# Causal attention and expert layer on one core: part of the diagonal mask as constant rows of the score product, and one f16 piece of the row maxima

## The chip, the cores and the metric

One Trainium2 chip, one core of it. The metric is the device time of one launch in microseconds (us). Each kernel is one program with one launch; 775.1 us is the median of three runs of the kernel before (772.79 to 777.4).

## What is computed

Eight batches of eight heads, 576 positions, head size 64, in f32; then a layer of eight experts with a capacity of 576 tokens each, routed by the largest remaining logit.

```python
scores = scale * np.matmul(q, k.transpose(0, 1, 3, 2))
causal = np.triu(np.ones((S, S), dtype=bool), k=1)
cum = np.cumsum(np.maximum(s, 0.0), axis=-1)
bias = -(cum[:, :, :, None] - cum[:, :, None, :])
scores = np.where(causal, -1000000000.0, scores + np.minimum(bias, 0.0))
scores = scores - np.max(scores, axis=-1, keepdims=True)
attn = np.exp(scores)
attn = attn / (np.sum(attn, axis=-1, keepdims=True) + 1e-09)
return np.matmul(attn, v).astype(np.float32)
...
logits = x @ w_gate          # x: the attention output, 4608 tokens of 512
h = np.maximum(x[mask] @ w1[e], 0.0)
out[mask] = h @ w2[e]        # for each expert e and the tokens given to it
```

## The kernel before

**Order of the work.** Every instruction is a task of a planner (class Plan, L90 on): it has an engine (t = TensorE, a = ScalarE, v = VectorE, p = GpSimd, s = the SyncE queue of transfers), a guessed duration, tasks that must come first, buffers from rings, and a priority (smaller goes first). The planner plays the engines through and gives out the instructions in the order in which they start in that play; each engine then runs its own list strictly in that order, waiting on semaphores. A change of one duration or one task so changes the order of the whole attention phase. Tasks marked `lock` are played so that one on VectorE and one on GpSimd don't overlap. A transfer marked `bulk` starts only when the backlog of transfers in the play (270 KB per us) has come down to 0.8 us. The expert phase has a plan of its own that the diff doesn't touch.

**Attention.** The 64 heads go in 16 groups g of four heads, each group in two pairs pr of two heads ("par" 0 and 1), so 32 pairs, numbered n0 = 2g + pr. For each group `load` (L363) brings q and k, scales them and splits them into a high and a low f16 part. They lie in one of four ring slots of the tile QK, `[128, 2, 2, 2, HB]` in f16 (partitions, plane, q or k, pair, 1280 columns). Partitions 0 to 63 of plane 0 hold the high parts; partitions 64 to 69 of plane 0 hold six more rows that enter the same product: three pieces of the running sums (the bias), two pieces of the row maximum and one constant. Plane 1 holds the cross products of high and low parts on all 128 partitions. Partitions 70 to 127 of plane 0 are not used.

**First pass** (`spass`, L459): scores from 67 rows of plane 0 alone, whose row maxima VectorE takes in ten steps (L471) into mr. The ten maxima of a row go through ScalarE as f16 into mp (L518) and as f32 into ms (L520); GpSimd takes the difference as the second f16 piece (L522); TensorE turns mp over (L524), ScalarE copies it out as mt of 20 rows (L526), and a transfer (L529) lays it into rows 67 and 68 of plane 0.

**Second pass** (`sts`, L533): the transposed scores, keys in the partitions and queries in the columns, 512 columns at a time (`unit`). Each piece of columns is one product over 70 rows of plane 0 (L544) plus one over 128 rows of plane 1 (L545), summed in PSUM; a block on the diagonal gets a third one, 128 columns of the identity times the mask mT (L547), which adds -1e9 where the key is later than the query:

```python
def mm(ps, c0, n, ks, q, diag=False):
    nc.tensor.matmul(ps[:, c0:c0 + n], F()[:, ks:ks + 128], F()[:, q:q + n], start=True, stop=False)
    nc.tensor.matmul(ps[:, c0:c0 + n], G()[:, ks:ks + 128], G()[:, q:q + n], start=False, stop=not diag)
    if diag:
        nc.tensor.matmul(ps[:, c0:c0 + 128], self.identb, self.mT, start=False, stop=True)
```

There are four diagonal blocks for each head: as the first 128 of 512, of 384 and of 256 columns, and one of 128 alone. ScalarE takes the exponential into P (L555), GpSimd writes what bf16 leaves of it into R (L557). `pv` (L592) multiplies with V in three products for each block (L618 to L620), `norm` (L631) divides (VectorE L644, L645, L649), `turn` (L662) transposes the result (L681) and adds it to the router logits (L692, L693). L411 and L444 are VectorE's low parts of q, k and v. At the start 70 products of zeros (L735) run on TensorE, and `consts` (L248) makes the constants, most of them on GpSimd.

**Experts.** After the last pair the router finishes, and eight experts run one after the other (lines from L840 on).

Of the kernel before, what the change touches and what calls it, by code (L numbers as in the profile page):

```python
# [42 lines left out]
OH = 704  # L43
# [173 lines left out]
class Attention:  # L217
# [30 lines left out]
    def consts(self):  # L248
# [17 lines left out]
        self.wgf = T([128, 4, E], F32, "wgf")  # L266
        self.vec = T([128, 2], F32, "vec")
# [10 lines left out]
        zrow = self.mZ.bitcast(F16)[64:70, None, 0:HB // 2].to_broadcast([6, 4, HB // 2])  # L278
        for i in range(4):
            t = self.r["QK"].slots[i][0]  # L280
            p0 = -97 if i == 0 else 2 * i - 5.6
            rows, made = t[64:70, 0], []
            if i < 2:
                for c in (1, 0):
                    made.append(pl.add("v", 0.85, lambda rows=rows, c=c: nc.vector.tensor_scalar(
                        rows[:, c].rearrange("p r (h c) -> p (r h) c", h=2), zrow, self.vec[64:70, c:c + 1], None,
                        op0=OP.add), [k["vec", 0, 4], k["vec", 1, 1], k["mZ"]], prio=p0 if c or i else -94, lock=True))
            else:

                made.append(pl.add("p", 0.9, lambda rows=rows: nc.gpsimd.dma_start(rows, self.r["QK"].slots[1][0][64:70, 0]),  # L290
                                   self.rows1 + [k["QK", 1]], prio=-20, kb=62))
# [167 lines left out]
    def spass(self, g, pr):  # L459
# [69 lines left out]
        st["max", pr] = pl.add("s", 0.67, lambda: nc.sync.dma_start(to.t[67:69, 0, 0, pr], mt.t), [x], prio=n0 - 2.9,  # L529
                               uses=[mt, QK], kb=5, alt=("a", 0.62, lambda: nc.scalar.dma_start(  # L530
                                   to.t[67:69, 0, 0, pr], mt.t)) if n0 < 4 else None)

    def sts(self, g, pr):  # L533
# [7 lines left out]
        ready = [k["ib"], k["mT1"], k["mU1", 0], k["mU1", 64], st["max", pr]] + st["pass"][pr][0] + st["pass"][pr][1] + st["st"][pr]  # L541
# [20 lines left out]
        for m, (par, j) in enumerate(((0, 0), (0, 1), (0, 2), (1, 0), (1, 1), (1, 2))):  # L562
            o, t = self.q0(par, pr, 0), self.q0(par, pr, 4) + 64 * par
            kk = lambda ki, par=par: self.k0(par, pr) + 128 * ki
            if j == 0:
                go = lambda ps, o=o, kk=kk: mm(ps, 0, 512, kk(0), o, True)
                dur = 2 * T_(512) + T_(128)
            elif j == 1:
# [4 lines left out]
                dur = 4 * T_(64) + 2 * T_(384) + T_(128)  # L573
            else:
# [5 lines left out]
                dur = 4 * T_(64) + 2 * T_(256) + 4 * T_(128)  # L580
# [136 lines left out]
    def build(self):  # L717
# [5 lines left out]
        self.sums()  # L723
        self.gate()
# [747 lines left out]
```

## Time and profile before

| what | value |
|---|---|
| three runs, median (lowest to highest) | 775.1 us (772.79 to 777.4) |
| the profiled execution's own time | 777.66 us |
| its span, first to last instruction | 775.6 us |
| TensorE (PE) busy | 722.0 us, 93% |
| VectorE (DVE) busy | 598.2 us, 77% |
| ScalarE (ACT) busy | 391.7 us, 50% |
| GpSimd (POOL) busy | 335.3 us, 43% |
| transfers | 118.72 MB, mean 153 GB/s |
| mean granted TensorE clock | 0.964 of 2.4 GHz |

A busy matmul in the profile includes the modelled time until its result has drained, so that successive matmuls overlap: their price is read from start to start. PEld is the loading of a matmul's weights, POOL is GpSimd, SPq the queue of the SyncE engine, from which most transfers are issued. Idle time in brackets is that of the engine just before the instruction, with what ended it.

### The profile page before, as it was taken

How to read it: one execution, taken by the hardware profiler on the slowest of the kernel's cores; microseconds unless marked ns; L12 is line 12 of the kernel's file. 1: busy time of each engine (PE TensorE's matmuls, PEld its weight loads, DVE VectorE, ACT ScalarE, POOL GpSimd, SP SyncE). 2: the span in 40 equal slices, each digit the busy share in tenths (PEclk: the TensorE clock that was granted, in tenths of full speed). 3: DMA queues.
4: the chain of work that ended last, by engine and by line, in shares of the span. 5: the costliest groups of instructions: out<-in, count | busy, mean ns of one | idle time of the engine just before them, and what ended most of it. 6: DMA issues, size and time to landing. Idle time of an engine off the chain costs nothing.

```text
span 775.6 us, 22590 instructions
## 1 busy us (share of the span) xinstructions
PE 722.0 (93%) x8726; PEld 454.9 (59%) x8726; DVE 598.2 (77%) x2014; ACT 391.7 (50%) x794; POOL 335.3 (43%) x428
## 2 busy tenths in 40 slices
PE   9789999999999999628998999999999999999995
PEld 3457788787888888416644544545445454454542
DVE  7889999999999996678895877969788795380110
ACT  3548888888888878405334323324244232461110
POOL 7648988788878988102032041140412224202011
PEclk9679999999999999858999999999999999999998
DMA  7897768686776511106157376394845639851000
GB/s 233 195 213 202 220 175 250 172 241 196 209 203 171 156 35 64 63 35 204 42 167 200 110 113 180 129 222 133 190 156 155 187 105 262 228 180 48 15 28 34
DMA packets 89733, 118.72 MB, mean 153 GB/s; under 512 B 39246, under 2 KB 55758, under 8 KB 89614
## 3 DMA queue, kind: packets, MB, share of 16 engines
q1 hardware_dynamic: 83116, 97.82, 46.1%
q0 software_dynamic: 5952, 19.00, 8.1%
q8 instruction: 68, 1.11, 0.6%
q10 hardware_dynamic: 558, 0.47, 0.2%
q14 instruction: 39, 0.32, 0.1%
HBM read 71.67 MB, written 19.10 MB: 117 GB/s over the span
## 4 chain that ended last, share of the span: by engine, by line
PE 54%; issue 19%; DVE 13%; DMA 5%; POOL 4%; ACT 2%; SPq 1%; POOLq 0%; ACTq 0%; DVEq 0%
PE psm L1293 13%; PE psm L1379 10%; DVE pss L471 5%; PE pst L545 4%; PE pst L544 4%; PE pss L502 3%; PE po L618 3%; PE po L620 2%; PE po L619 2%; POOL out_dram L1352 2%; POOL xg L1226 2%; PE psn L1297 2%; PE po L735 2%; PE pss L681 2%; DMA xg<-xs,ids 1%
## 5 line engine op out<-in xcount | busy, mean ns | idle before, releaser
L557 POOL TENSOR_TENSOR R<-P 128x512 f16<-128x512 f32 (+1 forms) x221 | 218.9, 1016 | 26.9 <-ACT P L555 25.2
L1293 PE MATMUL psm<-xT,w1p 128*128 128x512 f16 (+1 forms) x876 | 193.1, 353 | 1.3 <-DMA xT<-xg 0.8
L1379 PE MATMUL psm<-w2p,hT 128*128 128x512 f16 x768 | 174.4, 379 | 0.0
L555 ACT ACTIVATE P<-pst 128x512 f32<-128x512 f32 (+1 forms) x224 | 119.9, 555 | 25.0 <-PE pst L547 10.3
L1297 PE MATMUL psn<-xT,w1p 128*128 128x64 f16 x768 | 129.7, 193 | 0.0
L471 DVE CUSTOM_DVE_ANT_0 pss<-pss,mS 128x512 f32<-128x512 f32 (+3 forms) x256 | 122.7, 506 | 9.0 <-PE pss L502 8.0
L1293 PEld LDWEIGHTS <-w1p 128*128 128x128 f16 x876 | 79.2, 98 | 80.0 <-issue 1.9
L1352 POOL DMA_INDIRECT out_dram<-y,ids x40 | 39.8, 995 | 198.7 <-ACT y L1390 169.6
L1379 PEld LDWEIGHTS <-hT 128*128 128x128 f16 x768 | 69.0, 98 | 80.3 <-issue 4.4
L1226 POOL DMA_INDIRECT xg<-xs,ids x40 | 43.6, 1089 | 167.3 <-DVE ids L1184 67.3
L618 PE MATMUL po<-V,P 128*128 128x65 f16 x960 | 113.8, 196 | 1.4 <-DVE xp L649 1.0
L620 PE MATMUL po<-V,R 128*128 128x65 f16 x960 | 114.0, 194 | 0.4 <-POOL R L557 0.4
L619 PE MATMUL po<-Vl,P 128*128 128x64 f16 x960 | 113.6, 193 | 0.0
L544 PE MATMUL pst<-QK 70*128 70x64 f16 (+4 forms) x512 | 108.5, 252 | 1.2 <-ACT P L555 0.7
L545 PE MATMUL pst<-QK 128*128 128x64 f16 (+4 forms) x512 | 107.8, 251 | 0.0
L619 PEld LDWEIGHTS <-P 128*128 128x128 bf16 x960 | 90.0, 100 | 9.1 <-issue 2.8
L618 PEld LDWEIGHTS <-P 128*128 128x128 bf16 x960 | 90.4, 98 | 5.9 <-issue 1.8
L1313 ACT ACTIVATE hT<-psm 128x512 f16<-128x512 f32 x64 | 38.2, 597 | 108.1 <-PE psm L1293 88.3
L620 PEld LDWEIGHTS <-R 128*128 128x128 f16 x960 | 89.9, 97 | 0.6 <-POOL R L557 0.6
L1390 ACT ACTIVATE y<-psm 128x512 f32<-128x512 f32 x32 | 19.1, 597 | 122.0 <-PE psm L1379 108.1
L502 PE MATMUL pss<-QK 67*128 67x512 f16 (+3 forms) x256 | 72.6, 307 | 4.7 <-DVE mr L471 2.4
L1297 PEld LDWEIGHTS <-w1p 128*128 128x128 f16 x768 | 67.7, 98 | 1.3
(221 smaller groups left out, 1443.4 us busy)
## 6 DMA issues: line engine op xcount, KB each, us to landing
QK<-QK SPq DMA_DIRECT2D x120, 144.0 KB
wst<-in_w_dram SPq DMA_DIRECT2D x32, 512.0 KB
wst<-in_w_dram SPq DMA_DIRECT2D x64, 256.0 KB
raw<-in_q_dram SPq DMA_DIRECT2D x32, 288.0 KB
raw<-in_k_dram SPq DMA_DIRECT2D x32, 288.0 KB
rv<-in_v_dram SPq DMA_DIRECT2D x32, 288.0 KB
xs<-xp SPq DMA_DIRECT2D x32, 256.0 KB
xs<-xp SPq DMA_DIRECT2D x8, 128.0 KB
```

Of the source, the lines that this page charges most:

```text
L471: return pl.add("v", dur, lambda: nc.vector.tensor_tensor_reduce(ps(), ps(), mask, 1.0, init() if init else -3e38, OP.add, OP.max, mr.t[:, ...
L502: nc.tensor.matmul(ps.t[:, :n], F()[:, q0:q0 + 128], F()[:, k0:k0 + n], start=True, stop=True)
L544: nc.tensor.matmul(ps[:, c0:c0 + n], F()[:, ks:ks + 128], F()[:, q:q + n], start=True, stop=False)
L545: nc.tensor.matmul(ps[:, c0:c0 + n], G()[:, ks:ks + 128], G()[:, q:q + n], start=False, stop=not diag)
L555: e = pl.add("a", n / 1200 + 0.171, lambda: nc.scalar.activation(P.t[:, c0:c0 + n], ps.t[:, :n], AF.Exp, scale=1.0 / YS), [x] + fresh, pri ...
L557: sub = lambda eng: eng.tensor_tensor(R.t[:, c0:c0 + n], P.t[:, c0:c0 + n], strided_hi(P.t)[:, c0:c0 + n], op=OP.subtract)
L618: nc.tensor.matmul(o[:, i], H[:, c:c + 128], V.t[:, pr, sl], start=f, stop=False)
L619: nc.tensor.matmul(o[:, i, 0:64], H[:, c:c + 128], Vl.t[:, pr, sl], start=False, stop=False)
L620: nc.tensor.matmul(o[:, i], R.t[:, c:c + 128], V.t[:, pr, sl], start=False, stop=l)
L1293: nc.tensor.matmul(ps[:, tiles[0]:tiles[-1] + 1] if len(tiles) > 1 else ps[:, tiles[0]], lhs(f, c, a), xT.t[:, tiles[0]:tiles[-1] + 1, 4 * ...
L1297: nc.tensor.matmul(pt.t[:, 64 * f:64 * f + 64], lhs(f, c, a), xT.t[:, 4, 4 * b + c, 0:64], start=s, stop=e)
L1379: nc.tensor.matmul(py.t, hT.t[:, f, a, 128 * i:128 * i + 128], w2p.t[:, f, b], start=f == 0 and k == 0, stop=f == 7 and k == 2)
```

## The change

From the fifth group on (g >= 4, 24 of the 32 pairs), partitions 72 to 127 of plane 0 hold constants in all four slots: on the key side 65504 where the row's number is smaller than the key's (mA), on the query side -65504 where row and query have the same number (mB). Their product, summed over these 56 rows, is about -4.3e9 wherever the key is later than one of the first 56 queries of a block. The diagonal 128 columns are now a product of their own over all 128 partitions of plane 0, the columns after them a second one over 70, and the mask product is left with the last 72 of its 128 columns. The constants are made by four GpSimd instructions and brought into the slots by 16 transfers of 56 partitions by 2 KB. In all 32 pairs the row maximum goes as one f16 piece: the f32 copy, the difference and the second row are gone. Partitions 64 to 71 instead of 64 to 69 are filled at the start, with one more select for each of two columns of vec.

```diff
+HUGE, MR = 65504.0, 72
...
-            mr=R(w, [128, 10], F32, "mr", 3), ms=R(w, [128, 10], F32, "ms", 2), mp=R(w, [128, 128], F16, "mp", 2),
-            mt=R(w, [20, 128], F16, "mt", 2),
+            mr=R(w, [128, 10], F32, "mr", 3), mp=R(w, [128, 128], F16, "mp", 2), mt=R(w, [10, 128], F16, "mt", 2),
...
+            P(("vec", c), 0.2, lambda v=v: g.affine_select(
+                v, v, pattern=[[0, 1]], base=5, channel_multiplier=-1, compare_op=OP.is_ge, fill=0.0), -99, [("vec", c, len(rows))])
...
+    def rows(self):
+
+        nc, pl, k, g = self.nc, self.pl, self.k, self.nc.gpsimd
+        x = None
+        for t, v, op, base, fill in ((self.mA, HUGE, OP.is_ge, 63 + MR - 64, 0.0), (self.mB, 0.0, OP.not_equal, MR, -HUGE)):
+            x = pl.add("p", 0.5, lambda t=t, v=v: g.memset(t, v), [x], prio=1.5)
+            x = pl.add("p", 0.6, lambda t=t, op=op, base=base, fill=fill: g.affine_select(
+                t, t, pattern=[[0, 4], [1, 128]], base=base, channel_multiplier=-1, compare_op=op, fill=fill), [x], prio=1.5)
+        for i in range(4):
+            q = self.r["QK"].slots[i][0][MR:128, 0]
+            made = []
+            for t, (src, o1) in enumerate(((self.mB, OH + 64), (self.mA, OH))):
+                for o in (0, o1):
+                    made.append(pl.add("s", 0.6, lambda q=q, t=t, o=o, src=src: nc.sync.dma_start(
+                        q[:, t, :, o:o + 512], src[MR:128].rearrange("p i c -> p (i c)")[:, None].to_broadcast([128 - MR, 2, 512])),
+                        [x], prio=2.5 + i, kb=115, bulk=True))
+            k["rows", i] = made
...
-        a2 = pl.add("a", 0.21, lambda: nc.scalar.activation(ms.t.rearrange("p (a b) -> p a b", a=2), both(), AF.Copy, scale=1.0 / YS), done,
-                    prio=n0 - 2.9, uses=[mr, ms])
-        p1 = pl.add("p", 0.2, lambda: nc.gpsimd.tensor_sub(mp.t[:, 10:20], ms.t, mp.t[:, 0:10]), [a1, a2], prio=n0 - 2.9, lat=0.35,
-                    uses=[ms, mp])
...
-                   [p1, k["i16b"]], prio=n0 - 2.9, uses=[ps, mp])
-        x = pl.add("a", 0.25, lambda: nc.scalar.activation(mt.t, ps.t.bitcast(F16)[0:20, 0:128], AF.Copy), [x], prio=n0 - 2.9,
+                   [a1, k["i16b"]], prio=n0 - 2.9, uses=[ps, mp])
+        x = pl.add("a", 0.25, lambda: nc.scalar.activation(mt.t, ps.t.bitcast(F16)[0:10, 0:128], AF.Copy), [x], prio=n0 - 2.9,
...
+        new = g >= 4
+        F1 = lambda: self.flat(QK.t, slice(0, 128), 0)
...
         def mm(ps, c0, n, ks, q, diag=False):
-            nc.tensor.matmul(ps[:, c0:c0 + n], F()[:, ks:ks + 128], F()[:, q:q + n], start=True, stop=False)
+            m = 128 if diag and new else 0
+            if m:
+                nc.tensor.matmul(ps[:, c0:c0 + m], F1()[:, ks:ks + 128], F1()[:, q:q + m], start=True, stop=False)
+            if n > m:
+                nc.tensor.matmul(ps[:, c0 + m:c0 + n], F()[:, ks:ks + 128], F()[:, q + m:q + n], start=not m, stop=False)
             nc.tensor.matmul(ps[:, c0:c0 + n], G()[:, ks:ks + 128], G()[:, q:q + n], start=False, stop=not diag)
             if diag:
-                nc.tensor.matmul(ps[:, c0:c0 + 128], self.identb, self.mT, start=False, stop=True)
+                z = 128 - MR if new else 0
+                nc.tensor.matmul(ps[:, c0 + z:c0 + 128], self.identb, self.mT[:, z:], start=False, stop=True)
...
+        TM = T_(128) - (0.0233 if new else 0.0)
+        TB = TM + (0.003 if new else 0.0)
```

In `sts` the planner's durations of the units with a diagonal block use TB and TM instead of T_(128), and the tasks of a group from the fifth on also wait for the constants of their slot.

## Rows read from the trace of the kernel before

**Rows 1.** Busy time by stretch: length, PE, PEld, DVE, ACT, POOL (counts), clock, DMA share, GB/s.
```profile
20.00:60.00 40.00, 32.42 (x326) 21.25 (x324) 34.94 (x105) 21.57 (x44) 22.41 (x31) 0.74 0.89 205
60.00:100.00 40.00, 39.00 (x756) 31.89 (x754) 39.19 (x134) 34.43 (x83) 34.72 (x38) 1.00 0.76 212
100.00:240.00 140.00, 138.28 (x2683) 113.89 (x2682) 137.85 (x455) 120.93 (x277) 114.14 (x128) 1.00 0.72 205
240.00:300.00 60.00, 60.00 (x1198) 49.86 (x1196) 54.85 (x188) 48.79 (x120) 51.59 (x58) 1.00 0.37 109
```
**Rows 2.** Matmuls of L524, one for each pair, counted in two stretches.
```profile
100.00:240.00 140.00, 3.50 (x16) 1.56 (x16) 1.00 0.72 205
240.00:300.00 60.00, 1.54 (x7) 0.68 (x7) 1.00 0.37 109
```
**Rows 3.** The chain of waits within 100 to 240 us, shares by line.
```profile
by line: DVE pss L471 11.7%; PE pst L545 9.8%; PE pst L544 9.6%; PE pss L502 9.0%; PE po L618 7.0%; PE po L620 6.3%; PE po L619 6.2%; issue 4.7%; DVE Vl L444 4.6%; PE pss L681 4.0%; DVE po L645 3.5%; DVE QK L411 3.3%; PE pss L486 3.3%; PE p
```
**Rows 4.** The chain of waits within 240 to 300 us, shares by line.
```profile
by line: PE pst L545 15.9%; PE pst L544 15.7%; PE pss L502 12.1%; PE po L618 11.5%; PE po L620 10.7%; PE po L619 10.6%; PE pss L681 7.0%; PE pss L486 5.6%; PE pst L547 5.2%; PE po L692 1.6%; PE po L693 1.3%; PE pst L588 0.7%; PE pst L587 0.
```
**Rows 5.** TensorE's timeline, 165 to 168 us: start, duration, instruction.
```profile
165.56 0.38 PE L544 MATMUL pst<-QK 70*128 70x512 f16 x1
165.78 0.38 PE L545 MATMUL pst<-QK 128*128 128x512 f16 x1
166.00 0.22 PE L547 MATMUL pst<-mT,identb 128*128 128x128 bf16 x1
...
167.15 0.44 PE L681 MATMUL pss<-ident,xp 128*128 128x128 f16 x5
167.43 0.19 PE L618 MATMUL po<-V,P 128*128 128x65 f16 x1
```
**Rows 6.** Groups by form, 100 to 240 us: count, busy us, mean ns, idle before.
```profile
L557 POOL TENSOR_TENSOR R<-P 128x512 f16<-128x512 f32 x96 | 102.3, 1090 | 9.2 <-ACT P L555 8.9
...
L411 DVE SCALAR_TENSOR_TENSOR QK<-raw,QK 128x1152 f16<-128x1152 f32 x16 | 22.9, 1433 | 0.0
...
L547 PEld LDWEIGHTS <-identb 128*128 128x128 bf16 x128 | 12.5, 98 | 6.5
...
L522 POOL TENSOR_TENSOR mp<-ms,mp 128x10 f16<-128x10 f32 x16 | 7.4, 460 | 16.6 <-ACT ms L520 11.3 <-PE pss L486 4.3 <-PE pst L545 1.0
...
L520 ACT ACTIVATE ms<-mr 128x10 f32<-128x10 f32 x16 | 3.3, 205 | 0.0
```
**Rows 7.** VectorE's timeline, 134 to 138 and 160 to 170 us.
```profile
135.18 1.67 DVE L444 SCALAR_TENSOR_TENSOR Vl<-rv,V 128x1152 f16<-128x1152 f32 x1
136.78 0.48 DVE L649 TENSOR_TENSOR xp<-po,xp 128x320 f16<-128x320 f32 x1
...
163.09 1.31 DVE L411 SCALAR_TENSOR_TENSOR QK<-raw,QK 128x1152 f16<-128x1152 f32 x1
```
**Rows 8.** TensorE's timeline at 137 us; in brackets the idle time before.
```profile
137.31 0.19 PE L618 MATMUL po<-V,P 128*128 128x65 f16 x1 [0.61 <-DVE xp L649]
```
**Rows 9.** GpSimd's timeline, 0 to 60 us.
```profile
12.70 1.76 POOL L831 TENSOR_SCALAR_AFFINE_SELECT qb<-on 128x128 f16<-128x128 f16 x4
...
21.46 0.21 POOL L522 TENSOR_TENSOR mp<-ms,mp 128x10 f16<-128x10 f32 x1 [6.14 <-ACT ms L520]
```
**Rows 10.** The chain of waits within 14 to 60 us: start, length, what.
```profile
13.79 2.16 PE po L735 x10
...
26.72 6.87 DMA QK<-QK
...
49.28 5.94 DMA raw<-in_q_dram
...
56.37 0.25 ACT mt L526
```
**Rows 11.** The SyncE queue's timeline, 55 to 57 us.
```profile
55.23 0.36 SPq L382 DMA_DIRECT2D raw<-in_k_dram  x1
55.86 0.96 SPq L440 DMA_DIRECT2D rv<-in_v_dram  x2
```

More of the change, by code (lines that the diff above doesn't have):

```diff
@@ L266, in consts @@
         self.wgf = T([128, 4, E], F32, "wgf")
+        self.mA, self.mB = T([128, 4, 128], F16, "mA"), T([128, 4, 128], F16, "mB")
         self.vec = T([128, 2], F32, "vec")
@@ L281, in consts @@
             p0 = -97 if i == 0 else 2 * i - 5.6
-            rows, made = t[64:70, 0], []
+            rows, made = t[64:MR, 0], []
             if i < 2:
@@ L285, in consts @@
                     made.append(pl.add("v", 0.85, lambda rows=rows, c=c: nc.vector.tensor_scalar(
-                        rows[:, c].rearrange("p r (h c) -> p (r h) c", h=2), zrow, self.vec[64:70, c:c + 1], None,
-                        op0=OP.add), [k["vec", 0, 4], k["vec", 1, 1], k["mZ"]], prio=p0 if c or i else -94, lock=True))
+                        rows[:, c].rearrange("p r (h c) -> p (r h) c", h=2), zrow, self.vec[64:MR, c:c + 1], None,
+                        op0=OP.add), [k["vec", 0], k["vec", 1], k["mZ"]], prio=p0 if c or i else -94, lock=True))
             else:
-                made.append(pl.add("p", 0.9, lambda rows=rows: nc.gpsimd.dma_start(rows, self.r["QK"].slots[1][0][64:70, 0]),
+                made.append(pl.add("p", 0.9, lambda rows=rows: nc.gpsimd.dma_start(rows, self.r["QK"].slots[1][0][64:MR, 0]),
                                    self.rows1 + [k["QK", 1]], prio=-20, kb=62))
@@ L509, in spass @@
                 extra.append(tri(9, At(ps, 384, 448), self.mC, 64, x, prio, more=[k["mC1", 0], k["mC1", 64]]))
-        ms, mp, mt, ps = (self.buf(n) for n in ("ms", "mp", "mt", "pst" if n0 < 2 else "pss"))
+        mp, mt, ps = (self.buf(n) for n in ("mp", "mt", "pst" if n0 < 2 else "pss"))
         fresh = [k["mp", n0]] if n0 < 2 else []
@@ L519, in spass @@
                     prio=n0 - 2.9, uses=[mr, mp])
-        a2 = pl.add("a", 0.21, lambda: nc.scalar.activation(ms.t.rearrange("p (a b) -> p a b", a=2), both(), AF.Copy, scale=1.0 / YS), done,
-                    prio=n0 - 2.9, uses=[mr, ms])
-        p1 = pl.add("p", 0.2, lambda: nc.gpsimd.tensor_sub(mp.t[:, 10:20], ms.t, mp.t[:, 0:10]), [a1, a2], prio=n0 - 2.9, lat=0.35,
-                    uses=[ms, mp])
         x = pl.add("t", 0.06, lambda: nc.tensor.transpose(ps.t.bitcast(F16)[:, 0:128], mp.t, self.ident16),
-                   [p1, k["i16b"]], prio=n0 - 2.9, uses=[ps, mp])
-        x = pl.add("a", 0.25, lambda: nc.scalar.activation(mt.t, ps.t.bitcast(F16)[0:20, 0:128], AF.Copy), [x], prio=n0 - 2.9,
+                   [a1, k["i16b"]], prio=n0 - 2.9, uses=[ps, mp])
+        x = pl.add("a", 0.25, lambda: nc.scalar.activation(mt.t, ps.t.bitcast(F16)[0:10, 0:128], AF.Copy), [x], prio=n0 - 2.9,
                    uses=[ps, mt])
         to = QK
-        st["max", pr] = pl.add("s", 0.67, lambda: nc.sync.dma_start(to.t[67:69, 0, 0, pr], mt.t), [x], prio=n0 - 2.9,
+        st["max", pr] = pl.add("s", 0.67, lambda: nc.sync.dma_start(to.t[67:68, 0, 0, pr], mt.t), [x], prio=n0 - 2.9,
                                uses=[mt, QK], kb=5, alt=("a", 0.62, lambda: nc.scalar.dma_start(
-                                   to.t[67:69, 0, 0, pr], mt.t)) if n0 < 4 else None)
+                                   to.t[67:68, 0, 0, pr], mt.t)) if n0 < 4 else None)
     def sts(self, g, pr):
@@ L540, in sts @@
         fresh = [k["P", n0], k["R", n0]] if n0 < 2 else []
-        ready = [k["ib"], k["mT1"], k["mU1", 0], k["mU1", 64], st["max", pr]] + st["pass"][pr][0] + st["pass"][pr][1] + st["st"][pr]
+        new = g >= 4
+        F1 = lambda: self.flat(QK.t, slice(0, 128), 0)
+        ready = (k["rows", g % 4] if new else []) + [k["ib"], k["mT1"], k["mU1", 0], k["mU1", 64], st["max", pr]] + st["pass"][pr][0] + st["pass"][pr][1] + st["st"][pr]
         def mm(ps, c0, n, ks, q, diag=False):
-            nc.tensor.matmul(ps[:, c0:c0 + n], F()[:, ks:ks + 128], F()[:, q:q + n], start=True, stop=False)
+            m = 128 if diag and new else 0
[3 more added lines that the diff above has]
+                nc.tensor.matmul(ps[:, c0 + m:c0 + n], F()[:, ks:ks + 128], F()[:, q + m:q + n], start=not m, stop=False)
             nc.tensor.matmul(ps[:, c0:c0 + n], G()[:, ks:ks + 128], G()[:, q:q + n], start=False, stop=not diag)
             if diag:
-                nc.tensor.matmul(ps[:, c0:c0 + 128], self.identb, self.mT, start=False, stop=True)
+                z = 128 - MR if new else 0
+                nc.tensor.matmul(ps[:, c0 + z:c0 + 128], self.identb, self.mT[:, z:], start=False, stop=True)
         T_ = lambda n: n / 2400 + 0.003
+        TM = T_(128) - (0.0233 if new else 0.0)
+        TB = TM + (0.003 if new else 0.0)
         st["e", pr] = {}
@@ L566, in sts @@
                 go = lambda ps, o=o, kk=kk: mm(ps, 0, 512, kk(0), o, True)
-                dur = 2 * T_(512) + T_(128)
+                dur = 2 * T_(512) + TB
             elif j == 1:
@@ L572, in go @@
                     mm(ps, 448, 64, kk(1), t)
-                dur = 4 * T_(64) + 2 * T_(384) + T_(128)
+                dur = 4 * T_(64) + 2 * T_(384) + TB
             else:
@@ L579, in go @@
                     mm(ps, 448, 64, kk(3), t)
-                dur = 4 * T_(64) + 2 * T_(256) + 4 * T_(128)
+                dur = 4 * T_(64) + 2 * T_(256) + 2 * T_(128) + TB + TM
             unit((par, j), (par * PW + 512 * j, 512), dur, go, [], n0 + m / 7)
@@ L723, in build @@
         self.sums()
+        self.rows()
         self.gate()
```

2 lines of the change are left out of this document (1 added, 1 removed).

## Prediction

> **What bounds the kernel now.** I read the busy time by stretch first [rows 1]: between 60 and 300 us TensorE is at full clock and nearly always busy, VectorE too up to 240 us, GpSimd at 82 to 87%; the stretch up to 60 us has the transfers at 89% of their engines and a clock of 0.74. Busy shares don't tell which of two full engines decides, so next comes the pace. Each pair has one L524, 16 in 140 us and 7 in 60 us [rows 2]: 8.75 us a pair up to 240 us, 8.57 us after. The chain of waits says why: after 240 us it consists of TensorE alone [rows 4]; up to 240 us [rows 3], of the shares that are shown, the TensorE lines make 55.2% and VectorE's (L471, L444, L645, L411) 23.1%. So 8.57 us is what TensorE needs for a pair, and the 0.18 us above it is waiting for VectorE. One such wait: GpSimd and VectorE hold each other up, a two-input step of VectorE takes 1.31 us when free and 1.67 us here, so the L649 behind it is late [rows 7], and the L618 that needs the buffer finds TensorE idle for 0.61 us [rows 8]. Before 60 us the chain runs through transfers [rows 10]. The expert phase isn't touched and only moves.
>
> **Shorter masks.** 24 pairs times 8 diagonal blocks are 192 mask products. In a stream a matmul costs its columns at 2.4 GHz and a little more: 512 columns start 0.22 us apart (213.3 ns of columns), five of 128 take 0.28 us, 56 ns each (53.3 ns) [rows 5]. Going from 128 to 72 columns takes off 56 columns, 23.3 ns, in all 4.48 us of TensorE.
>
> **Split products.** Three of the four diagonal blocks of a head are cut off from a longer product, so 24 x 2 x 3 = 144 matmuls are new, with no new columns. Each costs the part above its columns, 2.7 ns by the 128-column row, 6.7 ns by the 512-column row [rows 5]; I take 5 ns, 0.72 us. Its weight load, 98 ns in its row [rows 6], must hide: the five transposes start 56 ns apart, each with weights of its own [rows 5], so loads overlap and I add nothing. 128 rows for 70 in the diagonal product: L544 over 70 rows and L545 over 128 rows both take 0.22 us from start to start [rows 5], so nothing. Net 3.76 us of TensorE (3.5 to 4.1), 0.157 us a pair.
>
> The row thus prices a 128-column matmul with its own weights at 56 ns. The Trainium skill (TensorE: Matmul & The Clock Gate, "Back-to-back issue gap") says that in a stream of weight loads and matmuls the spacing is set by both, about 81 ns at 128 columns and 131 ns at 512, which would make the splits dear; the trace disagrees at both ends, with 56 and 220 ns.
>
> **What of it reaches the end.** The eight pairs 24 to 31 run where the chain is TensorE alone: 8 x 0.157 = 1.25 us. Of the 16 changed pairs before them, which run in about the stretch of [rows 3] (2.51 us), I count two thirds, about TensorE's part of the chain (55.2 of 78.3) with something off for VectorE, which is then late sooner: 1.67 us. Together 2.9 us. The ends are 1.25 us (nothing where VectorE stands on the chain) and 3.76 us (all).
>
> **One piece of the maxima.** ScalarE loses L520, 0.205 us a pair [rows 6]; it is at 86% [rows 1] and on no chain that I show above, so nothing. GpSimd loses L522, 0.46 us a pair with its waits, and 1.04 us a pair of standing idle ahead of it while the R of L557, 1.09 us each, queue behind [rows 6]. No row shows TensorE waiting for an R, so directly nothing. Indirectly it moves when GpSimd and VectorE collide: L411 took 1.433 us on average against 1.31 us free [rows 6, 7], 16 x 0.123 = 2.0 us of blocking between 100 and 240 us; that can go or double, and nothing says which: 0, with 2.0 us either way in the range. The shorter way to the row of maxima could matter only before 60 us, where the chain is transfers [rows 10]: 0; at most the 0.205 + 0.46 us of the two steps for each of the first four pairs, 2.7 us.
>
> **Another order.** New durations and missing tasks shift every engine's list. The 16 x 0.18 = 2.9 us above TensorE's pace is what an order can give back or lose again: 0, with 2.9 us either way.
>
> **Constants.** Four GpSimd instructions: four selects of 128 columns take 1.76 us [rows 9], so a select of 512 about as much, and a fill no more: under 7.0 us, nearer 4. Their priority 1.5 puts them ahead of the router's constants (3), whose end is followed by 6.14 us of idle GpSimd [rows 9]: hidden; uncovered it would cost up to 0.9 us. The two selects for vec, at most 0.44 us each by the same row, stand ahead of the first loads' rows; the chain at 14 us is still in the zero products of L735 [rows 10], so hidden, 0 to 0.9 us.
>
> **Sixteen transfers.** 56 rows x 2 x 1 KB are 0.115 MB, in all 1.84 MB. From 60 to 100 us the transfers move 212 GB/s at a share of 0.76 [rows 1], so full engines would move 279 GB/s and need 6.6 us for them; the free 24% of those 40 us is 9.6 us. From 20 to 60 us, at 0.89, only 4.4 us are free, and at that stretch's 205 GB/s over 0.89 they need 8.0 us. Which stretch? The first slot's priority is 2.5; the q and k of the fifth group (1.0) and the v of the fourth (1.5) go first, and these were issued at 55.23 and 55.86 us [rows 11]; the other slots (3.5 and later) also stand behind the sixth group's q and k (3.0). So after 57 us, ahead of the first use, in the ninth pair: 0. The price if not is a rival below. On SP each issue is some 0.4 us and waits for constants long made.
>
> **Sum.** 777.66 - 2.9 = 774.8 us against the profiled execution's own time, which lies 2.56 us above the median of the runs; from the median, 772.2 us.
>
> **Rivals.**
> *VectorE paces.* It is busy 98% of 100 to 240 us [rows 1], and nothing is taken off it. Then only the last eight pairs gain: 775.1 - 1.25 = 773.9 us. Against: some of that busy time is blocking, and TensorE leads the chain.
> *The blocking goes too.* Without L522 GpSimd and VectorE collide less, and the first 16 pairs come down to TensorE's new pace: 16 x (0.18 + 0.157) + 1.25 = 6.6 us, 768.5 us. For: the 16.6 us of idle ahead of L522 [rows 6]. Against: L557 blocks as before.
> *Slower, by the transfers.* Place: 20 to 60 us. Constants are ready early, and where the planner's 270 KB per us empties a backlog that the chip still has, rows go out ahead of q, k and v. The chain there is a QK transfer of 6.87 us and a load of 5.94 us, behind which ScalarE's queue held L526 up to 56.37 us [rows 10]. Price: 8.0 - 4.4 = 3.6 us of transfers too many, up to all 8.0 us if they stand ahead of the load on the chain. It decides from 2.9 us on, what the masks give; at 6 us it is 775.1 + 3.1 = 778.2 us. A TensorE idle longer there also stays at the half clock longer.
> *Slower, by weight loads.* If the 98 ns of a load [rows 6] stood open for each of the 144 splits, 14.1 us would go against 4.48 us: 784.7 us. The 56 ns of [rows 5] speak against it. By the page named above the splits would also cost more than the masks give.
> *Not what it says.* 65504 squared over the scale of 8192 is an exponent near -520,000, so the mask holds and the time is as summed.
>
> **How the numbers follow.** Forecast 45% (its own range 770.3 to 774.5); VectorE paces 20%; blocking goes 17%; transfers 14%; weight loads 2%; 2% for an order that is worse by more. What a measurement of this kernel can tell from no change is about 0.5%, 3.9 us: under 771.2 or over 779.0 us. Under it lie a third of the forecast's spread by reordering (15%), nearly all of the case without blocking (16%) and a little of the rest (5%): 0.36. Over it lie over half of the transfers' case (8%) and the last two (4%): 0.12. The range takes in the gain without blocking and part of what early transfers cost: 767.5 to 778.0 us.
>
> **What would show it.** After 240 us the pace falls from 8.57 to 8.41 us a pair and the mask products are 33 ns apart (72 columns and 3 ns); in 100 to 240 us it falls to about 8.65 us, with VectorE still on the chain. The sixteen transfers are issued after 57 us and the chain before 60 us is as it was. It is wrong if the pace after 240 us stays, if diagonal products of 128 columns start much over 58 ns apart, if the first 60 us grow by microseconds, or if the pace before 240 us falls by more than TensorE's 0.157 us.

## Result and profile after

| | kernel before | changed kernel |
|---|---|---|
| four runs each, median (lowest to highest) | 776.12 us (772.79 to 777.4) | 784.92 us (783.43 to 785.89) |
| ratio, 95% interval | | 1.0118 (1.008 to 1.0156) |
| the profiled execution's own time, its span | 777.66, 775.6 us | 783.43, 781.7 us |
| mean granted clock | 0.964 | 0.964 |

The change makes the kernel slower by 1.2%, against a forecast of 772.2 us and a range that ended at 778.0. The spans differ by 6.1 us. The lines of the changed kernel have moved: L471 is L492, L411 and L444 are L432 and L465, L502 is L523, L524 is L541, L544 is L567 with the new L565 over 128 rows, L545 is L568, L547 is L571, L557 is L583, L618 to L620 are L644 to L646, L649 is L675, and the 16 transfers are L339.

Busy time by stretch of the changed kernel (length, PE, PEld, DVE, ACT, POOL with counts, clock, DMA share, GB/s), the same stretches as in [rows 1]:

```profile
20.00:60.00 40.00, 29.57 (x374) 19.51 (x373) 32.56 (x119) 22.55 (x45) 24.30 (x38) 0.83 0.79 197
60.00:100.00 40.00, 36.82 (x669) 29.55 (x666) 35.57 (x118) 29.91 (x66) 29.98 (x33) 0.96 0.65 186
100.00:240.00 140.00, 134.06 (x2686) 111.53 (x2683) 134.56 (x433) 114.83 (x255) 116.42 (x108) 1.00 0.76 212
240.00:300.00 60.00, 58.88 (x1205) 49.69 (x1202) 58.42 (x206) 47.98 (x110) 50.65 (x49) 1.00 0.47 134
```

TensorE stood idle for 1.7 us of 100 to 240 us before, now for 5.9 us; after 240 us it was never idle, now for 1.1 us. In 100 to 240 us VectorE and ScalarE are less busy too, and no engine is full in TensorE's place; after 240 us VectorE is busier than before, 97%. The chain of waits, shares by line, first 100 to 240 us, then 240 to 300 us:

```profile
by line: DMA raw<-in_q_dram 10.1%; DVE QK L432 8.6%; DVE pss L492 8.6%; issue 7.3%; PE pss L523 7.2%; PE pst L568 7.0%; PE po L644 5.1%; PE pst L567 4.8%; PE po L646 4.5%; PE po L645 4.4%; DMA rv<-in_v_dram 4.1%; PE pss L507 3.2%; PE pss L7
...
by line: DVE pss L492 13.5%; PE pst L568 10.6%; PE pss L523 9.4%; PE po L644 7.9%; PE po L646 7.3%; PE po L645 7.3%; PE pst L567 7.2%; PE pss L507 4.4%; PE pss L707 3.8%; PE pst L565 3.5%; DVE po L671 2.8%; DVE L L733 2.4%; DVE mr L492 2.3%
```

Before, the second of these was TensorE alone [rows 4] and the shown part of the first named no load [rows 3]. Now VectorE leads the last stretch and loads of q stand at the head of the one before it.

**A clock for the pairs.** The last products of every pair, and only those, take the constant mU (L589 before), two for each pair. The row that groups them from pair 8's first to pair 31's last, 48 products and so 23 pairs apart, gives the pace of all pairs that the change touches but the first. In the kernel before:

```profile
L589 PE MATMUL pst<-mU,identb x48: 190/190/191, 117.0 to 313.3; 128*128 128x64 bf16 x48
```

and in the changed kernel:

```profile
L615 PE MATMUL pst<-mU,identb x48: 190/190/191, 118.6 to 319.7; 128*128 128x64 bf16 x48
```

196.3 us became 201.1 us. Pair 8 ends 1.6 us later, the 23 pairs add 4.8 us, and with that the 6.1 us of the span are told: what follows pair 31 took 462.3 us before and 462.1 us after. "23 pairs" is this figure from here on; pairs' lengths are the differences of these marks.

**Where in the 23 pairs.** Pairs 7 to 14 keep level: pair 7 ends at 107.88 us before and 106.73 after, so the opening with its transfers is not the loss, and pair 14 at 169.60 and 170.67. Pair 17 ends at 196.50 and 203.60, 7.1 us behind, and pair 31 still 6.4 behind. The busy time of 150 to 185 us in the kernel before:

```profile
150.00:185.00 35.00, 34.83 (x681) 28.81 (x680) 34.36 (x117) 30.80 (x71) 27.62 (x33) 1.00 0.76 214
```

and in the changed kernel, with 5 us out of it:

```profile
165.00:170.00 5.00, 4.72 (x121) 4.26 (x119) 5.00 (x5) 2.06 (x7) 0.97 (x1) 1.00 0.82 211
...
150.00:185.00 35.00, 31.71 (x590) 25.33 (x587) 33.52 (x99) 25.61 (x58) 26.68 (x25) 1.00 0.74 208
```

TensorE issued 590 matmuls where it had issued 681. Within, VectorE spends 165 to 170 us on five instructions, while ScalarE is busy for 2.1 us of these and GpSimd for 1.0. Its timeline there (start, duration, instruction) names them:

```profile
163.83 1.35 DVE L465 SCALAR_TENSOR_TENSOR Vl<-rv,V 128x1152 f16<-128x1152 f32 x1
165.10 2.62 DVE L432 SCALAR_TENSOR_TENSOR QK<-raw,QK 128x1152 f16<-128x1152 f32 x2
167.64 1.35 DVE L465 SCALAR_TENSOR_TENSOR Vl<-rv,V 128x1152 f16<-128x1152 f32 x1
168.91 1.35 DVE L432 SCALAR_TENSOR_TENSOR QK<-raw,QK 128x1152 f16<-128x1152 f32 x1
```

Five low parts run in a row; before, no more than two stood together after 60 us. In those 6.4 us no maximum and no normalisation is made, and (the two engines being planned apart there) no R up to 169.03 us. GpSimd's timeline has the hole:

```profile
169.03 8.59 POOL L583 TENSOR_TENSOR R<-P 128x512 f16<-128x512 f32 x7 [5.95 <-ACT P L581]
```

TensorE is hardly idle beside them (4.72 us busy of 165 to 170 us); it misses 1.4 us in 160 to 165 us, mostly ahead of them, and 0.9 us in 175 to 180 us. Behind the last low part the chain of waits (start, length) goes on with a load of q, and only after its landing with ScalarE and TensorE:

```profile
171.72 5.10 DMA raw<-in_q_dram
```

**The new products themselves** cost what was forecast. TensorE's timeline of the changed kernel in a full stream:

```profile
158.82 0.22 PE L565 MATMUL pst<-QK 128*128 128x128 f16 x1
158.87 0.22 PE L567 MATMUL pst<-QK 70*128 70x128 f16 x1
158.93 0.27 PE L568 MATMUL pst<-QK 128*128 128x256 f16 x1
159.04 0.19 PE L571 MATMUL pst<-mT,identb 128*128 128x72 bf16 x1
159.07 0.19 PE L567 MATMUL pst<-QK 70*128 70x64 f16 x1
```

128 columns over 128 rows: 0.05 us to the next start, 128 over 70 rows 0.06 us; the mask product of 72 columns: 0.03 us.

### The profile page after: what moved, and what is told of

Its sections match the earlier page's. It is cut to its first block, busy times and chain, and to the rows that moved or that the text cites. A ratio compares the mean times of both kernels' runs of the same rounds, so it can differ in the third digit from the quotient of the medians.

```text
span 781.7 us, 22785 instructions
## 1 busy us (share of the span) xinstructions
PE 718.9 (92%) x8870; PEld 455.2 (58%) x8870; DVE 599.4 (77%) x2016; ACT 386.6 (49%) x762; POOL 338.4 (43%) x400
## 4 chain that ended last, share of the span: by engine, by line
PE 49%; issue 20%; DVE 16%; DMA 7%; POOL 4%; ACT 2%; SPq 1%; POOLq 0%; DVEq 0%; ACTq 0%
PE psm L1320 12%; PE psm L1406 10%; DVE pss L492 5%; PE pst L568 3%; DVE QK L432 3%; DMA raw<-in_q_dram 3%; PE pss L523 2%; PE po L644 2%; PE pst L567 2%; POOL out_dram L1379 2%; PE po L646 2%; PE po L645 2%; PE po L762 2%; PE psn L1324 2%; POOL xg L1253 1%
## 5 line engine op out<-in xcount | busy, mean ns | idle before, releaser
L583 POOL TENSOR_TENSOR R<-P 128x512 f16<-128x512 f32 (+1 forms) x220 | 232.5, 1084 | 57.1 <-ACT P L581 54.8
L492 DVE CUSTOM_DVE_ANT_0 pss<-pss,mS 128x256 f32<-128x256 f32 (+3 forms) x256 | 123.3, 506 | 10.4 <-PE pss L523 9.0
L644 PE MATMUL po<-V,P 128*128 128x65 f16 x960 | 109.6, 195 | 2.0 <-DVE xp L675 1.5
L646 PE MATMUL po<-V,R 128*128 128x65 f16 x960 | 109.8, 193 | 0.0
L645 PE MATMUL po<-Vl,P 128*128 128x64 f16 x960 | 109.4, 192 | 0.0
L568 PE MATMUL pst<-QK 128*128 128x64 f16 (+4 forms) x512 | 102.3, 249 | 0.0
L567 PE MATMUL pst<-QK 70*128 70x64 f16 (+4 forms) x464 | 98.8, 236 | 2.7 <-DMA QK<-mt 2.7
L644 PEld LDWEIGHTS <-P 128*128 128x128 bf16 x960 | 89.8, 98 | 4.4 <-issue 0.5
L646 PEld LDWEIGHTS <-R 128*128 128x128 f16 x960 | 89.2, 97 | 0.0
L523 PE MATMUL pss<-QK 67*128 67x128 f16 (+3 forms) x256 | 73.5, 304 | 9.5 <-DVE mr L492 5.2
```

The source lines that it names most:

```text
L492: return pl.add("v", dur, lambda: nc.vector.tensor_tensor_reduce(ps(), ps(), mask, 1.0, init() if init else -3e38, OP.add, OP.max, mr.t[:, ...
L523: nc.tensor.matmul(ps.t[:, :n], F()[:, q0:q0 + 128], F()[:, k0:k0 + n], start=True, stop=True)
L567: nc.tensor.matmul(ps[:, c0 + m:c0 + n], F()[:, ks:ks + 128], F()[:, q + m:q + n], start=not m, stop=False)
L583: sub = lambda eng: eng.tensor_tensor(R.t[:, c0:c0 + n], P.t[:, c0:c0 + n], strided_hi(P.t)[:, c0:c0 + n], op=OP.subtract)
L644: nc.tensor.matmul(o[:, i], H[:, c:c + 128], V.t[:, pr, sl], start=f, stop=False)
L645: nc.tensor.matmul(o[:, i, 0:64], H[:, c:c + 128], Vl.t[:, pr, sl], start=False, stop=False)
```

## Experiments

Two theories stood at first: the change's own work costs something that was priced at nothing (transfers, splits, one piece), or the order does that the planner made of it.

**The new work in the order of before, and the reverse.** e1 lets the planner see the tasks and durations of the kernel before, so that its lists stay, and puts the new instructions in; the transfers follow SyncE's own from a planned 52 us on, one behind each. e2 does the reverse: planned as the change, with the old instructions.

```diff
 e1
+        if self.extra and x.e == "s" and t >= self.extra_from:
+            self.extra.pop(0)()
...
+        a2 = pl.add("a", 0.21, lambda: None, done, prio=n0 - 2.9, uses=[mr, ms])
+        p1 = pl.add("p", 0.2, lambda: None, [a1, a2], prio=n0 - 2.9, lat=0.35, uses=[ms, mp])
...
+        TM = T_(128)
+        TB = TM
 e2
+            x = pl.add("p", 0.5, lambda: None, [x], prio=1.5)
...
+        def pieces():
+            nc.scalar.activation(mp.t[:, 0:10].rearrange("p (a b) -> p a b", a=2), both(), AF.Copy, scale=1.0 / YS)
+            nc.scalar.activation(ms.rearrange("p (a b) -> p a b", a=2), both(), AF.Copy, scale=1.0 / YS)
+            nc.gpsimd.tensor_sub(mp.t[:, 10:20], ms, mp.t[:, 0:10])
```

> All the work of the change (masks, split products, sixteen transfers, one piece of the maxima), but the planner is given the tasks and durations of the kernel before, so that every engine's list is that of before, with the new instructions put in. Theory 'order' (the new work saves what the sum said, and the loss is the other order of the lists): 772 to 775 us, 2 to 4 us under the kernel before, no run of more than two low parts on VectorE after 60 us. Theory 'work' (the transfers or the new products themselves cost the time): 780 us or more.

> The reverse: the planner is given the tasks and durations of the changed kernel, so the lists stand in its order, but the instructions are the old ones: 128-column masks, whole products, no constants, no transfers, two pieces of the maxima. Theory 'order': 783 to 790 us, as slow as the changed kernel or a few us slower, with the five low parts in a row near 164 us. Theory 'work': 775 to 779 us, as the kernel before.

e1: 784.73 us, ratio 1.0112 (1.0071 to 1.0152). e2: 795.63 us, 1.026 (1.0231 to 1.0288). Both halves cost, but e1 not where the change does. Its 23 pairs take 195.1 us, 1.2 less than before; the loss lies ahead, in pairs 4 and 6, each 6 us longer than before. Busy time of e1:

```profile
75.00:80.00 5.00, 1.07 (x9) 0.42 (x6) 1.10 (x7) 2.64 (x6) 0.91 (x1) 0.79 0.83 218
80.00:85.00 5.00, 5.00 (x42) 3.38 (x41) 2.48 (x12) 2.69 (x8) 5.00 (x6) 0.53 0.42 131
```

and its SyncE queue (start, issue time):

```profile
68.41 0.83 SPq L338 DMA_DIRECT2D QK<-mA  x1
69.35 0.76 SPq L549 DMA_DIRECT2D QK<-mt  x1
70.15 0.83 SPq L338 DMA_DIRECT2D QK<-mB  x1
71.03 0.67 SPq L404 DMA_DIRECT2D raw<-in_k_dram  x1
```

The issue of a transfer of constants holds SyncE for 0.83 us, and in this list loads queue behind it: TensorE stops, and its clock falls to 0.53 for the next 5 us. So e1's loss belongs to where e1 put the transfers. The 1.2 us that it gains later is the change's real work. By its time alone e1 would have spoken for the theory 'work', and e2 lies above what either theory expected: the places of the loss decide here, not the times.

**The two halves of the change, planned freely.** e3 keeps two pieces, e4 has one piece and no masks or constants.

```diff
 e3, against the changed kernel
+        p1 = pl.add("p", 0.2, lambda: nc.gpsimd.tensor_sub(mp.t[:, 10:20], ms.t, mp.t[:, 0:10]), [a1, a2], prio=n0 - 2.9, lat=0.35,
+                    uses=[ms, mp])
 e4, against the changed kernel
-        self.rows()
...
-        TM = T_(128) - (0.0233 if new else 0.0)
-        TB = TM + (0.003 if new else 0.0)
```

> The masks with their constants and transfers, but still two pieces of the maxima; the planner orders anew. Theory 'order': its lists have runs of three low parts at two places instead of one run of five, so 775 to 783 us, by its waits for VectorE and not by the number of transfers. Theory 'work' by transfers: the same transfers as the changed kernel, so 782 us or more.

> One piece of the maxima, masks and transfers as before; the planner orders anew. Its lists have no run of more than two low parts after 40 us. Theory 'order': 773 to 779 us. Theory 'holes' (without the difference GpSimd runs its R without a break, shuts VectorE's low parts out, and that alone costs the time): 781 us or more, with the low parts bunched.

e3: 792.18 us, 1.0233 (1.0196 to 1.0271), 23 pairs 206.9 us. e4: 782.66 us, 1.0096 (1.0066 to 1.0127), 201.3 us. The halves cost 2.3% and 1.0%, the whole 1.2%: they don't add, as prices of instructions would. Both are slower than was expected of the order (775 to 783 and 773 to 779 us), and e4 loses without a run of low parts after 40 us.

**Nothing changed but the order.** e5 is e1 with the transfers placed two behind each row of maxima from the fifth pair on. e6, e7 and e8 run the old instructions: e6 believes the masks shorter, e7 believes each matmul longer by 0.1 ns, e8 a hop between engines longer by 0.1 ns.

```diff
 e5, against e1
+            for _ in range(2 if n0 >= 4 else 0):
+                if pl.extra:
+                    pl.extra.pop(0)()
 e6, against the kernel before
+        TM = T_(128) - (0.0233 if g >= 4 else 0.0)
+        TB = TM + (0.003 if g >= 4 else 0.0)
 e7
-        T_ = lambda n: n / 2400 + 0.003
+        T_ = lambda n: n / 2400 + 0.0031
 e8
-    HOP = 0.04
+    HOP = 0.0401
```

> As e1 (all the work of the change in the order of before), but the sixteen transfers are no longer given out one after each transfer from 52 us on: two follow the transfer of the row maxima of each pair from the fifth on, so they spread over some 60 us, each slot's before its first use. Theory 'queue' (e1 lost its 10 us between 74 and 100 us because sixteen issues of 0.83 us crowded the SyncE queue and the row maxima came late; the masks and the one piece save 3 to 4 us): 771 to 775 us, with no wait of TensorE over 1.5 us between 60 and 300 us. Theory 'work' (the transfers cost their time wherever they stand): 780 us or more.

> The kernel before with not one instruction changed; only the planner believes that the masks take what the changed kernel's take, so that the order differs. Theory 'lucky order' (the order of before is better than what its planner gives out for nearly equal guesses): 779 to 790 us. Theory 'order is harmless' (it costs only where low parts are shut out, and is else within a measurement): 773 to 779 us, or up to 781 us for its one run of four low parts late in the phase.

> The kernel before with not one instruction changed; the planner's guess for each product of the second pass is 0.1 ns longer. Theory 'lucky order': 779 to 790 us. Theory 'order is harmless': 773 to 779 us.

> The kernel before with not one instruction changed; the planner's guess for the signal between engines is 40.1 ns in place of 40.0, which changes the lists from the sixth pair or so on, without a longer run of low parts than before has. Theory 'lucky order': 777 to 785 us. Theory 'order is harmless': 773 to 779 us.

| run | us | ratio (95%) | 23 pairs, us |
|---|---|---|---|
| e5, new work, order of before | 774.61 | 1.0028 (1.0005 to 1.0051) | 195.4 |
| e6, old work, another order | 779.7 | 1.0101 (1.008 to 1.0122) | 203.0 |
| e7, old work, another order | 779.65 | 1.0101 (1.006 to 1.0142) | 204.2 |
| e8, old work, order of before in the attention | 771.18 | 0.9976 (0.996 to 0.9991) | 196.3 |

This decides between the two theories. All the change's work, in the order of before, takes 195.4 us for the 23 pairs, 0.9 less than before, and pair 8 is 1.05 us longer, 0.6 us of it a wait of TensorE for one of the transfers: nothing on net in these 24 pairs. Over the whole kernel e5 is still 0.28% above before (0.05 to 0.51%); the marks show no place for that. The part behind pair 31 has the same lists in all runs but e8 and took between 459.5 and 465.4 us in their traces, so a difference of some us in a time says less than the 23 pairs do.

The old work in two other orders, e6 and e7, loses 1%. e8 was meant as a third, but its longer hop left the attention as it was: up to 342 us every engine has the same instructions in the same order as before, and only the router and the experts behind are reordered. (So a changed guess need not change the attention's order.) For the attention e8 is a repeat of before, and shows how well the marks repeat: 196.25 against 196.27 us. Its 0.24% lie behind pair 31, 456.4 us against 462.3. e6 loses most at one place, pairs 27 and 28, 5.74 and 17.65 us long (8.55 each before); VectorE's timeline there:

```profile
284.05 1.35 DVE L444 SCALAR_TENSOR_TENSOR Vl<-rv,V 128x1152 f16<-128x1152 f32 x1
285.32 2.62 DVE L411 SCALAR_TENSOR_TENSOR QK<-raw,QK 128x1152 f16<-128x1152 f32 x2
287.86 1.35 DVE L444 SCALAR_TENSOR_TENSOR Vl<-rv,V 128x1152 f16<-128x1152 f32 x1
```

Four low parts in a row, and GpSimd's timeline again has the hole:

```profile
291.26 6.03 POOL L559 TENSOR_TENSOR R<-P 128x512 f16<-128x512 f32 x6 [7.29 <-ACT P L557]
```

e7 has three in a row at 268.3 us and a fourth just ahead, with two short steps between, and its pairs 26 and 27 take 13.07 and 12.29 us.

**Are the runs of low parts the cause?** A low part is put off in the plan as long as GpSimd's R have the shared time (`lock`); put off together, they come together. A bound on that wait should break the runs up: 24 us and 12 us, in the changed kernel (e9, e10) and in the two null orders (e11, e12).

```diff
 e9, e10 (12.0), against the changed kernel; e11 (24.0), against e7; e12 (12.0), against e6
-            t = max(t, self.port["p" if e == "v" else "v"])
+            other = self.port["p" if e == "v" else "v"]
+            t = max(t, min(other, x.ready + 24.0) if e == "v" else other)
```

> The changed kernel, with one more rule in the planner: a low part of VectorE that has been ready for 24 us may start although GpSimd stands in its way, so that low parts can't be shut out and then come in a row. No instruction is added or taken away; the lists have no run of more than two low parts after 20 us. Theory 'bunched low parts' (the loss of the changed kernel is the run of five near 164 us and the pairs behind it): 770 to 779 us, over 5 us under the changed kernel's 785, and no pair over 11 us long after the tenth. Theory 'any new order costs' : 780 to 790 us.

> The same with 12 us in place of 24: a third order, again without a run of more than two low parts after 40 us. Theory 'bunched low parts': 768 to 779 us. Theory 'any new order costs': 780 to 790 us.

> e7 (the kernel before, the guess for each product 0.1 ns longer) with the same rule at 24 us, which takes away its run of three low parts late in the phase and leaves one of two. Theory 'bunched low parts': the 6.7 us that e7 lost come back, 770 to 776 us. Theory 'any new order costs': 779 us or more, as e7.

> e6 (the kernel before, not one instruction changed, the masks believed shorter) with the rule at 12 us: the old work in an order without runs of low parts after 30 us. Theory 'bunched low parts': 768 to 776 us, under e6's 779.7. Theory 'any new order costs': 779 us or more. Beside e10, the same rule with the change's own work: if the masks reach the end, e10 is the faster one by up to 3.8 us; if VectorE paces once the order is good, within 1.5 us of it.

e9: 784.1 us, 1.0094 (1.0063 to 1.0124). e10: 788.64, 1.0133 (1.0083 to 1.0184). e11: 783.45, 1.0105 (1.0046 to 1.0165). e12: 781.65, 1.0066 (1.0036 to 1.0095). In none of the four do more than two low parts stand together after 20 us, and the time doesn't come back: the 23 pairs take 201.1 us in e9, like the change's, and 206.3, 205.1 and 200.9 us in e10, e11 and e12. TensorE is busy for 173.5 us of 120 to 300 us in e9, before for 178.6 us; its waits there (total us, times, longest), of which before had three of together 1.0 us, are many and short, most of them for VectorE:

```profile
PE po L645 <- DVE xp L676: 1.7, 3, 1.1
PE po L719 <- DVE xp L676: 1.5, 2, 0.9
PE pss L542 <- ACT mp L540: 0.5, 1, 0.5
```

The theory falls as the general cause. That a run of low parts is one way in which an order is bad is argued from the places alone: no run takes such a run away and leaves the rest of the order as it was.

**The halves in the order of before.** With the order held, what is each half worth, and how dear are the transfers? e13 is e5 with both pieces kept and three transfers behind each row of maxima, e14 only the one piece, e15 is e5 with three transfers.

```diff
 e13 and e15, against e5
-            for _ in range(2 if n0 >= 4 else 0):
+            for _ in range(3 if n0 >= 4 else 0):
 e14, against the kernel before (and the opposite in e13, against e5)
-        p1 = pl.add("p", 0.2, lambda: nc.gpsimd.tensor_sub(mp.t[:, 10:20], ms.t, mp.t[:, 0:10]), [a1, a2], prio=n0 - 2.9, lat=0.35,
-                    uses=[ms, mp])
+        p1 = pl.add("p", 0.2, lambda: None, [a1, a2], prio=n0 - 2.9, lat=0.35, uses=[ms, mp])
```

> The order of before, with the masks, the split products and the sixteen transfers (three behind each transfer of the maxima from the fifth pair on), but the maxima still in two pieces, so GpSimd's list is that of before. Theory 'collisions' (e5 gave its masks' gain back where GpSimd, without the difference, ran its R at other moments and caught VectorE's two-input steps): this one keeps the gain, 770 to 774 us if before is 775, that is 2 to 4 us under it, and its pairs 22 to 28 take no longer than before's 60.2 us. Theory 'VectorE paces': within 1.5 us of before, pairs 22 to 28 as before, no gain even with the difference kept.

> The order of before, old masks, no transfers; only the maxima go in one piece. Theory 'collisions': 0 to 2 us over before, its pairs 22 to 28 about 1 us longer, with a two-input step of VectorE (the sum of the router's logits) held up near 236 us. Theory 'one piece is free': within 0.5 us of before, pairs 22 to 28 as before.

> e5 with three transfers behind each transfer of the maxima in place of two, so that the last is issued before the ninth pair's second pass. If e5's 0.7 us wait of that pass for a transfer was worth its length, 0.5 to 1 us under e5's ratio of 1.0028 to before, so a ratio of 1.000 to 1.003; if the SyncE queue is crowded by three already, 1.005 or more.

| run | us | ratio (95%) | pair 8 | 23 pairs | pair 23 | pair 28 |
|---|---|---|---|---|---|---|
| before | | | 9.22 | 196.3 | 10.69 | 8.55 |
| e13, masks | 781.21 | 1.0076 (1.0049 to 1.0104) | 14.62 | 194.7 | 10.73 | 8.50 |
| e14, one piece | 774.97 | 1.0003 (0.9987 to 1.002) | 9.06 | 196.8 | 11.52 | 9.26 |
| e5, both | 774.61 | 1.0028 (1.0005 to 1.0051) | 10.27 | 195.4 | 11.55 | 9.32 |
| e15, both | 783.7 | 1.0102 (1.0067 to 1.0138) | 16.84 | 195.1 | 11.55 | 9.32 |

Masks gain 1.6 us in the 23 pairs, one piece loses 0.5 us, and the 0.9 us that both gain together is near the sum. The halves also repeat the comparison of orders: the masks' work takes 194.7 us here and 206.9 us in e3's order, the one piece 196.8 us here and 201.3 us in e4's. By time e13 misses the 770 to 774 us that were expected of it, by its transfers; its pairs 22 to 28 take 59.7 us against 60.2 before, as 'collisions' expected, and e14's take 61.7 us. The sixteen transfers, three behind each row of maxima, cost 5.4 and 7.6 us at pair 8. How they do it, in e15: SyncE's queue,

```profile
111.36 0.78 SPq L548 DMA_DIRECT2D QK<-mt  x1
112.19 0.84 SPq L336 DMA_DIRECT2D QK<-mA  x1
113.16 0.38 SPq L417 DMA_DIRECT2D QK<-auxk  x1
```

ScalarE's timeline,

```profile
115.28 1.16 ACT L429 ACTIVATE QK<-raw 128x1152 f16<-128x1152 f32 x1 [5.35 <-DMA QK<-auxk]
...
116.45 1.55 ACT L587 ACTIVATE P<-pst 128x512 f32<-128x512 f32 x3
```

and TensorE's:

```profile
117.08 0.26 PE L571 MATMUL pst<-QK 128*128 128x128 f16 x1 [4.16 <-ACT P L587]
```

In e8, whose list is that of before, the same two issues are

```profile
102.32 0.69 SPq L529 DMA_DIRECT2D QK<-mt  x1
106.35 0.26 SPq L397 DMA_DIRECT2D QK<-auxk  x1
```

SyncE had 3.3 us to spare between them. In e15 fifteen issues of constants, 13.2 us in all, go ahead of that row of maxima, more than SyncE had spare: it is issued 9.0 us later than in e8, the transfer of auxk 6.8 us later. ScalarE's next instruction waits for it, the exponentials wait behind that, and TensorE behind them.

## Why the prediction was wrong

**The step that failed is "Another order": "0, with 2.9 us either way".** The 2.9 us were the time above TensorE's pace that the order of before still held. That bounds what another order can give back; it bounds nothing of what another can lose, and I used it for both. Measured: the changed kernel's 23 pairs take 201.1 us, the same work in the order of before 195.4 us (e5), so the new order costs 5.7 us, and old work, 196.3 us in the order of before, takes 203.0, 204.2 and 214.2 us in others (e6, e7, e2). The same planner drew five orders of the attention besides that of before (the change's, which e2 shares, and those of e3, e4, e6 and e7), and four more with the bound on the wait (e9 to e12): all nine take 201 to 207 us for the 23 pairs, each with the work that it was planned for. The order of before stands at the far end of these, so a redrawn one had to be expected to lose. I had written that a changed duration changes the whole order, and still gave an order "that is worse by more" 2%.

What makes a list good is only partly settled. Runs of three to five low parts stand at the places where the change, e6 and e7 lose most; lists without them (e4, e9 to e12) lose as much, e9 in many small waits. The cause within a list stays open.

**Shorter masks and splits: the price was right.** A mask product of 72 columns takes 0.03 us, the diagonal product of 128 columns that is split off 0.05 us, and with the order held, pairs 25 to 27 of e13 take 8.42 to 8.51 us against 8.55, where 8.41 was forecast; the last three pairs are 0.15 to 0.19 us shorter each, where 0.157 was. No weight load shows: that rival falls.

**What of it reaches the end: 2.9 us forecast, 1.6 us measured (e13).** Of 1.25 us in the last eight pairs 0.87 came, of 1.67 us in the others 0.75, without pair 8, which holds the transfers. The step took off a little, from 0.70 to two thirds, for a VectorE that is late sooner, and nothing in the last eight pairs; that was too little. In e13's chain from 123 to 240 us the maxima of VectorE (L492) have 16.5%, in that of before (L471) 10.7%: "VectorE paces" was half right. In the change itself VectorE leads the chain after 240 us, and its last eight pairs take 64.5 us against 64.4.

**One piece: 0 forecast, +0.5 us measured (e14), within the 2.0, and half of it not where I looked.** Two pairs pay, pair 23 with 0.83 us and pair 28 with 0.71 us. In pair 23 it isn't a low part that collides with an R, but the group's step on the router's logits (L707). In e14, VectorE and then GpSimd:

```profile
234.93 1.10 DVE L704 TENSOR_TENSOR L<-L,L 128x40 f32<-128x40 f32 x1
```

```profile
231.30 7.03 POOL L554 TENSOR_TENSOR R<-P 128x512 f16<-128x512 f32 x7 [0.66 <-ACT P L552]
```

and the same in e8:

```profile
237.19 0.27 DVE L707 TENSOR_TENSOR L<-L,L 128x40 f32<-128x40 f32 x1
```

```profile
233.82 0.58 POOL L522 TENSOR_TENSOR mp<-ms,mp 128x10 f16<-128x10 f32 x1 [0.93 <-ACT ms L520]
234.37 6.38 POOL L557 TENSOR_TENSOR R<-P 128x512 f16<-128x512 f32 x7
```

In both lists the small step, which adds two tiles, comes while one R follows the other without a break, and it ends 0.06 us behind an R: in e8 it starts 0.21 us before that R's end, in e14 together with a new R, and so it waits for all of it. Without the difference ahead of them the R start at other moments, and the step meets a whole one: 1.10 us for 0.27. In pair 28 it is the collision that the forecast had named, an R and a low part. VectorE in e14 and, the same instruction, in e8:

```profile
279.53 2.16 DVE L443 SCALAR_TENSOR_TENSOR Vl<-rv,V 128x1152 f16<-128x1152 f32 x1
```

```profile
280.97 1.33 DVE L444 SCALAR_TENSOR_TENSOR Vl<-rv,V 128x1152 f16<-128x1152 f32 x1
```

In e14 it starts 0.09 us behind an R; in e8 0.08 us ahead of one, and there that R takes 2.16 us for 1.03. Pairs 15, 18 and 21 of e14 are 0.4, 0.3 and 0.4 us shorter; by what is not shown. The Trainium skill (SBUF — State Buffer, "Who interferes with whom") says that a VectorE instruction with two inputs in SBUF contends with a GpSimd instruction that reads SBUF, and that the later of the two blocks fully. The 1.10 us and the two times 2.16 us agree.

**Constants: right.** In the changed kernel a fill takes 0.52 to 0.60 us and a select 0.64 to 0.73 us, at 8.3 to 10.9 us, under the zero products.

**Transfers: nearly right in place, wrong in size.** In the change one goes out early and fifteen after 57 us, as forecast; SyncE's queue, those begun before 60 us and the last:

```profile
18.55 0.99 SPq L339 DMA_DIRECT2D QK<-mB  x1
...
58.15 0.92 SPq L339 DMA_DIRECT2D QK<-mB  x1
59.12 1.71 SPq L339 DMA_DIRECT2D QK<-mA  x2
...
78.19 0.81 SPq L339 DMA_DIRECT2D QK<-mA  x1
```

Pair 2 ends at 60.65 us before and 59.97 after, and pair 7 no later either: the rival that put the loss into 20 to 60 us falls. But "some 0.4 us" for an issue was taken from a load [rows 11]; these take 0.81 to 0.99 us but for one, 14.5 us of SyncE for the sixteen. My price was bandwidth in a busy stretch; the one that the runs show is the queue, and it depends on the place: 1 us in e5, 5 to 12 us in e1, e13 and e15.

**Chances and range.** The three signs had 0.36, 0.52 and 0.12. The last, the one that came, was built from transfers (0.08), weight loads (0.02) and an order that is worse by more (0.02); the mechanism that decided had a sixth of it, and in the sum its price was cut off at 2.9 us.

## What to carry to other kernels

Where a planner or a compiler draws the order anew, a change is two changes: the instructions, and the order. Price the second by null changes (a guessed duration moved by 0.1 ns) before trusting a gain of half a per cent, and compare the lists first: of three here one left the attention's lists alone, and the two that redrew them cost 1.0% each. All nine redrawn orders lost against that of before; how that one was come by, no run shows. To learn what the instructions are worth, hold the old order and put the new work into it; and price a transfer by what it holds on its queue, from a row of its own shape, not by its bytes alone.

## What the runs showed that was not expected

- A list of the same instructions for the attention phase, redrawn after a change of 0.1 ns in one guessed duration, costs 7.9 us over the 23 pairs (e7), while the same list twice (before and e8) agrees to 0.02 us.
- In another list the same edit is worth another sum: old to new work in the order of the change takes the 23 pairs from 214.2 to 201.1 us, in the order of before from 196.3 to 195.4 us.
- Issue on SyncE differs by shape: in the first 320 us of the changed kernel the medians are 0.44 us for a load of k (single ones from 0.33 to over 2 us), 0.60 us for a move within QK, 0.79 us for the row of maxima and 0.81 us for 56 partitions of 2 KB, spread from one source. The row of maxima in one piece holds SyncE longer than in two (0.69 us in the kernel before).
